# Shorter table steps, float64 pieces split by ScalarE and VectorE, and other first and last steps of the last layer

## The chip, the cores and the metric

The kernel runs on one core of a Trainium2 chip. The core has a matrix engine (TensorE, PE in the profile; its weight loads are PEld), a vector engine (VectorE, DVE), a scalar engine (ScalarE, ACT), a general engine (GpSimd, POOL), a queue engine that issues most of the transfers (SyncE, SP), and 16 DMA engines that all queues share. The metric is the device time of one execution in microseconds; lower is better. The kernel before takes 802.15 us (median of three runs, 800.84 to 803.86).

## The reference

Three layers follow each other. The first is clustered attention, which the change does not touch. Its output is a table x of 1536 tokens by 512 numbers. The second sends every token to the one expert of eight that its gate prefers. The third multiplies two projections and projects the product.

```python
logits = x @ w_gate                                  # 1536 x 8
expert_idx = np.argmax(logits, axis=1)
for e in range(8):
    xe = x[expert_idx == e]
    h = np.maximum(xe @ w1[e], 0.0)                  # 512 -> 1024
    out[mask] = gate_w[mask, None] * (h @ w2[e])     # 1024 -> 512
a, b = out @ w_a, out @ w_b                          # w_a, w_b, w_out are float64, 512 -> 1536
result = (a * b @ w_out).astype(np.float32)          # 1536 -> 512
```

The layer of experts is given in float32 and the last layer's weights in float64. The kernel keeps float32 accuracy with matmuls on shorter numbers: every operand is split into a high part and the rest (hi and lo, hh and hl, xh and xl, yh and yl), and three products hi·hi, hi·lo and lo·hi are added up.

## The kernel before

**Weights as pieces.** All weights come in pieces, in one list. A piece is loaded by SP into one of four buffers called raw (L102 for an expert's piece, L104 for a float64 one; 512 KB each). ScalarE casts it to hi (L138), and then raw − hi is lo (L142), computed by DVE for expert pieces of 128 x 1024 and by POOL for float64 ones of 128 x 512. A float64 piece first has its bits put together into float32 by three DVE operations (L121, L123, L125, into tmp, two buffers). The function `advance(n, engines, later)` takes the pieces up to number n through this path; with later = 1 the bits are made one piece ahead. A load of a piece is issued when the piece four places ahead has been passed on. Pieces 0 to 71 are the experts' (nine windows of eight pieces), numbers from 72 up are the last layer's. The list `chunk_src` gets an expert's pieces only once the registers that name the expert have been read.

**Windows.** The experts' work is nine windows, in an order that depends on the counts of tokens. The windows are 256 tokens long (`window`), but the fourth and the sixth run 128 tokens in another form (`tile_of`). A window has eight h groups (12 matmuls each, L1067; the results go to one of three PSUM banks, and hh by ScalarE and hl by DVE, L1072, set the bank free) and eight groups of y (L1082) into one buffer; at the end ScalarE and DVE each copy half of y to yt (L1090, L1091). Before a window, its tokens are fetched (xw, L1043), transposed on PE (xt, L1052) and split into xh and xl (L1055, L1056); the transposes of the next window stand between the y groups of this one.

**What sets the order.** The program is written out, and each engine takes its instructions in that order. `tick()` is called 16 times in a window, after each hl and before each y group; it counts t, runs one step of the tables if it is due, starts the second window's weights and tokens at t = 1, and calls `advance` up to a number that grows with t. The tables (a Python generator that stops at each yield) turn the counts of tokens into the order of the experts (`ri`, L659 to L674), the second kind of window (`wi`, L704) and the places of the tokens (`pu`, L767), for which POOL scatters `aux` (L769, twelve of them in two sets of six; each writes 128 rows of two words). Before, steps run at t = 0 to 3 and then, from t = 24, only in the second half of each window.

**Behind the windows** stands a loop (L1270) whose number of passes is read from the tables; it makes none here, but all engines meet at it. Then comes the last layer: 12 steps in a group, each with 24 matmuls into ab (L1354), the product ga, its split gh (L1362) and gl (L1363), and matmuls into four tiles o (L1377). Before each step `advance` takes the float64 pieces that it needs. At the end of the last group DVE adds up each tile's o to part (L1385) and POOL scatters it to the output (L1388). In the last group the tile t = 3 has the matmuls of its last two steps behind the three other tiles' ones.

The functions that the change touches, and their callers:

## Time and profile before

The profiled execution took 800.87 us, and its span (first to last instruction) is 799.1 us.

| what | value |
|---|---|
| runs | 803.86, 802.15, 800.84 us |
| profiled execution, its span | 800.87 us, 799.1 us |
| mean granted TensorE clock | 0.987 |
| PE busy | 766.6 us (96%) |
| DVE busy | 530.7 us (66%) |
| ACT busy | 356.1 us (45%) |
| POOL busy | 171.5 us (21%) |
| attention ends, experts begin | about 281 us |
| first to seventh window begin | 281.0, 310.4, 334.4, 357.7, 377.2, 401.0, 416.0 us |
| ninth window begins | 462.4 us |
| boundary with the loop, last layer | 487.6 to 499.5, 499.5 to 791.5 us |

The granted clock is a share of full speed: 1.00 is 2.4 GHz and half of it 1.2 GHz. The busy share of PE is high, but it is a mean over stages; where PE stands still is found by its waits and by stage.

### The profile page before, as it was taken

What the parts mean: (1) busy time and instruction counts of PE and PEld (TensorE: products, weight loads), DVE (VectorE), ACT (ScalarE), POOL (GpSimd) and SP (SyncE); (2) the same over time, 40 slices, a digit from 0 to 9 for tenths busy, and PEclk for the clock granted to TensorE, in tenths of its full rate; (3) what the DMA queues carried; (4) which work ended last, traced back from release to release, by engine and by line L of the source; (5) the groups of instructions that cost most, each with busy time, mean ns of one, the idle gap of its engine ahead of it and who ended that gap; (6) DMA issues with size and microseconds to landing.
All of it is one profiled execution on the core that took longest, in us unless ns stands there. A gap on an engine that the chain in (4) does not pass through costs nothing. (4 is left out here: it accounts for less than half of the span.)

```text
span 799.1 us, 12580 instructions
## 1 busy us (share of the span) xinstructions
PE 766.6 (96%) x4725; PEld 632.6 (79%) x4725; DVE 530.7 (66%) x939; ACT 356.1 (45%) x677; POOL 171.5 (21%) x172
## 2 busy tenths in 40 slices
PE   9999999999999889997999996999999999999996
PEld 8667666675666779996999986788888888888884
DVE  5877868868686787875776687856556665625332
ACT  6767667665675456455575532232241221211100
POOL 7533231414210400011300033312112111101011
PEclk9999999999999999999999998999999999999999
DMA  6585953855410268669997644413121230001011
GB/s 140 140 212 167 290 123 95 195 102 156 100 40 1 73 217 284 206 195 201 219 289 227 200 138 132 132 53 105 53 53 53 57 103 0 1 1 53 1 53 53
DMA packets 76302, 98.17 MB, mean 123 GB/s; under 512 B 28368, under 2 KB 49360, under 8 KB 76240
## 3 DMA queue, kind: packets, MB, share of 16 engines
q1 hardware_dynamic: 73792, 91.01, 41.6%
q0 software_dynamic: 2304, 6.31, 2.1%
q8 instruction: 38, 0.62, 0.3%
q14 instruction: 24, 0.20, 0.1%
q10 hardware_dynamic: 144, 0.03, 0.0%
HBM read 70.32 MB, written 10.50 MB: 101 GB/s over the span
## 5 line engine op out<-in xcount | busy, mean ns | idle before, releaser
L1354 PE MATMUL ab<-yh,hi 128*128 128x512 f32 x288 | 113.2, 393 | 6.5 <-ACT yh L1326 6.5
L1354 PE MATMUL ab<-yh,lo 128*128 128x512 f32 x288 | 113.0, 392 | 0.0
L1361 DVE TENSOR_TENSOR ga<-ga,ab 128x512 f32<-128x512 f32 x36 | 24.7, 685 | 127.3 <-PE ab L1354 104.4
L142 POOL TENSOR_TENSOR lo<-tmp,hi 128x512 fp32r<-128x512 f32 x36 | 51.6, 1433 | 247.6 <-ACT hi L138 245.6
L461 DVE TENSOR_REDUCE nm<-s 128x1 f32<-128x768 f32 x96 | 91.5, 953 | 18.2 <-PE s L459 11.3
L142 DVE TENSOR_TENSOR lo<-raw,hi 128x1024 fp32r<-128x1024 f32 x70 | 85.0, 1223 | 25.0 <-ACT hi L138 24.1
L468 ACT ACTIVATE pr<-s,nm 128x768 f32<-128x768 f32 x96 | 86.9, 905 | 18.3 <-DVE nm L461 16.3
L459 PE MATMUL s<-ks,qs 128*128 128x512 f32 (+1 forms) x384 | 91.6, 361 | 0.3 <-ACT pr L468 0.3
L482 PE MATMUL t<-ident,pr 128*128 128x128 f32 x576 | 82.8, 277 | 3.8 <-DVE pt L488 2.3
L1360 ACT COPY ga<-ab 128x512 f32<-128x512 f32 x36 | 21.1, 585 | 143.3 <-PE ab L1354 143.3
L482 PEld LDWEIGHTS t<-ident,pr 128*128 128x128 f32 x576 | 64.6, 141 | 25.1 <-issue 10.9
L138 ACT CAST hi<-raw 128x1024 fp32r<-128x1024 f32 x70 | 72.2, 1046 | 17.0 <-DMA raw<-in_moe_w 17.0
L1354 PE MATMUL ab<-yl,hi 128*128 128x512 f32 x288 | 77.3, 390 | 0.0
L498 PE MATMUL o<-pt,vn 128*64 128x384 f32 (+1 forms) x432 | 74.5, 468 | 0.0
L488 DVE COPY pt<-t 128x384 f32<-128x384 f32 x94 | 51.9, 552 | 27.2 <-PE t L482 27.0
L1354 PEld LDWEIGHTS ab<-yh,hi 128*128 128x128 f32 x288 | 54.6, 190 | 18.1 <-ACT yh L1326 6.7
L486 ACT COPY pt<-t 128x384 f32<-128x384 f32 x98 | 46.8, 479 | 46.6 <-PE t L482 43.8
L459 PEld LDWEIGHTS s<-ks,qs 128*128 128x128 f32 x384 | 58.5, 190 | 9.7 <-issue 4.4
L1082 PE MATMUL y<-hh,hi 128*128 128x256 f32 x224 | 64.1, 286 | 0.0
L1354 PEld LDWEIGHTS ab<-yh,lo 128*128 128x128 f32 x288 | 54.7, 190 | 11.3
L1354 PEld LDWEIGHTS ab<-yl,hi 128*128 128x128 f32 x288 | 54.5, 189 | 11.4
L1082 PE MATMUL y<-hh,lo 128*128 128x256 f32 x224 | 63.2, 282 | 0.0
(327 smaller groups left out, 1559.3 us busy)
## 6 DMA issues: line engine op xcount, KB each, us to landing
raw<-in_moe_w SPq DMA_DIRECT2D x72, 512.0 KB, 4.7
raw<-in_moe_w_a SPq DMA_DIRECT2D x12, 512.0 KB, 4.1
raw<-in_moe_w_b SPq DMA_DIRECT2D x12, 512.0 KB, 4.0
raw<-in_moe_w_out SPq DMA_DIRECT2D x12, 512.0 KB, 3.2
qs<-hiq SPq DMA_DIRECT2D x14, 384.0 KB
ks<-hik SPq DMA_DIRECT2D x28, 192.0 KB, 4.4
xs<-zero SPq DMA_DIRECT2D x8, 512.0 KB
xw<-xs SPq DMA_DIRECT2D x14, 256.0 KB, 3.7
```

The lines of the kernel that those rows point to most:

```text
L138: nc.scalar.copy(out=hi, in_=raw)
L142: eng.tensor_tensor(out=lo, in0=raw, in1=hi.bitcast(F32), op=ALU.subtract)
L459: nc.tensor.matmul(sc[:, c0:c1], lhsT=w, rhs=ks[s, h][:, i, c0:c1], start=(i == 0), stop=(i == 1))
L461: nc.vector.tensor_reduce(out=nm, in_=sc[:, 0:S], axis=AX.X, op=ALU.max, negate=True)
L468: nc.scalar.activation(out=pr, in_=sc[:, 0:S], func=AF.Exp, bias=nm, scale=1.0, accum_out=sums[p][:, t, h:h + 1])
L482: nc.tensor.transpose(x[:, 128 * n:128 * n + 128], pr[:, 128 * kb:128 * kb + 128], ident)
L486: nc.scalar.copy(out=dst, in_=src)
L488: nc.vector.tensor_copy(dst, src)
L498: nc.tensor.matmul(o[64 * h:64 * h + 64, 0:n], lhsT=vn[:, h, kb, :], rhs=pt_t[p, g, h][:, kb, 128 * j0:128 * j0 + n], start=(kb == 0), sto ...
L1082: nc.tensor.matmul(y[:, d, 0:n], lhsT=a_[:, fb % 2, 128 * d:128 * d + 128], rhs=b_[:, 0:n], start=(fb == 0 and d % 2 == 0 and i == 0), sto ...
L1354: nc.tensor.matmul(p_, lhsT=a_[:, d, f0:f0 + 128], rhs=b_[d], start=(i == 0), stop=(i == len(seq) - 1))
L1361: nc.vector.tensor_tensor(out=ga, in0=ga, in1=ab[1], op=ALU.mult)
```

## The change

Five parts, all in the order in which work is written out:

- The generator of the tables has eight more yields, so its steps are shorter, and one step runs at every tick from t = 0 on. The second window's weights and tokens are started at t = 4 and no longer at t = 1. The pieces of the experts lead by t // 8, not t // 4 (up to the same bound). In the first window the second window's transposes stand behind the y groups 3 and 5, not 1 and 3.
- The float64 pieces before the loop are eight, not nine. They are made at eight ticks listed in WHEN64, counted from t = T64 = 122, by `split_ahead`: bits on DVE, hi on ScalarE, and lo on DVE, one piece behind the hi.
- `held` bounds the loads before the last layer.
- In the first group of the last layer the pieces of a step are bounded by min(n64, 10 + step * 15 // 11 − (step == 0)); gh and gl have three buffers.
- In the last group, the last tile's matmuls of step GF − 3 also go behind those of the other tiles, so 9 of its matmuls stand there and no longer 6.

The diff, cut to what matters (the other yields are like the two shown):

```diff
--- before.py
+++ after.py
@@ -129,15 +129,18 @@
     def piece_parts(n, hi_eng, lo_eng):
-        raw = bits_t.pop(n)
+        raw = bits_t.pop(n) if lo_eng else bits_t[n]
         i, j = pieces[n]
         hi, lo = hi_t[i], lo_t[i]
         if i >= MOE2:
             hi, lo = (x[:, CH // 2 * j:CH // 2 * j + CH // 2] for x in (hi, lo))
         if hi_eng == "act":
             nc.scalar.copy(out=hi, in_=raw)
-        else:
+        elif hi_eng:
             nc.vector.tensor_copy(hi, raw)
+        if not lo_eng:
+            return
         eng = nc.gpsimd if lo_eng == "pool" else nc.vector
         eng.tensor_tensor(out=lo, in0=raw, in1=hi.bitcast(F32), op=ALU.subtract)
@@ -649,12 +652,15 @@
         e1 = cp.tile([128, E], F32, name="we1")
         od = tp.tile([128, E], F32, name="od")
         nc.vector.tensor_reduce(out=m[:, 0:1], in_=cnt[:, 1:E], axis=AX.X, op=ALU.min)
+        yield
         nc.vector.scalar_tensor_tensor(out=e1[:, 1:E], in0=cnt[:, 1:E], scalar=m[:, 0:1], in1=efirst[:, 0, 1:E],
                                        op0=ALU.is_le, op1=ALU.mult)
         nc.vector.tensor_reduce(out=m[:, 1:2], in_=e1[:, 1:E], axis=AX.X, op=ALU.max)
+        yield
         nc.vector.tensor_scalar(out=m[:, 2:3], in0=m[:, 1:2], scalar1=-1.0, scalar2=float(E), op0=ALU.mult, op1=ALU.add)
         nc.vector.scalar_tensor_tensor(out=od, in0=ecol, scalar=m[:, 2:3], in1=ecol, op0=ALU.is_ge, op1=ALU.add)
         nc.vector.tensor_copy(od[:, E - 1:E], m[:, 2:3])
+        yield
         ri = tp.tile([128, 3, E], I32, name="ri")
         nc.vector.tensor_copy(ri[:, 0, :], od)
         nc.vector.tensor_scalar(out=ri[:, 1, :], in0=od, scalar1=float(NTOK), scalar2=None, op0=ALU.mult)
@@ -1005,6 +1015,10 @@
     pools["b"] = pb
     st_me = ExitStack()
     mp = pool(st_me, "moe")
+    LAST64 = 8
+    held = [True]
     nload = [NA + NRAW]
     nsplit = [NA]
     nparts = [NA]
@@ -1023,6 +1037,21 @@
         while later and nsplit[0] < n:
             first_part()
+    def split_ahead(n):
+        if nparts[0] < MOE2:
+            advance(MOE2, ENG)
+        while nsplit[0] < n:
+            i = nsplit[0]
+            first_part()
+            piece_parts(i, "act", None)
+            if i > MOE2:
+                piece_parts(i - 1, None, "dve")
+                nparts[0] = i
+        if n == MOE2 + LAST64 and nparts[0] < n:
+            piece_parts(n - 1, None, "dve")
+            nparts[0] = n
     def first_part():
         i = nsplit[0]
         piece_bits(i)
@@ -1031,7 +1060,8 @@
             load_ahead(nsplit[0])
     def load_ahead(n):
-        while nload[0] < min(len(pieces), n + NRAW) and pieces[nload[0]] in chunk_src:
+        most = MOE2 + LAST64 + NRAW if held[0] else len(pieces)
+        while nload[0] < min(most, n + NRAW) and pieces[nload[0]] in chunk_src:
             piece_load(nload[0])
             nload[0] += 1
@@ -1055,7 +1085,7 @@
         nc.scalar.copy(out=oh, in_=xv)
         nc.vector.tensor_tensor(out=ol, in0=xv, in1=oh.bitcast(F32), op=ALU.subtract)
-    def window(w, n, c0, tick, nxt=None):
+    def window(w, n, c0, tick, nxt, at):
         hh, hl = [], []
         y = mps.tile([128, DB, W], F32, tag="y", name=f"y{w}")
         for fb in range(FB):
@@ -1082,8 +1112,8 @@
                     nc.tensor.matmul(y[:, d, 0:n], lhsT=a_[:, fb % 2, 128 * d:128 * d + 128], rhs=b_[:, 0:n],
                                      start=(fb == 0 and d % 2 == 0 and i == 0),
                                      stop=(fb == FB - 1 and d % 2 == 1 and i == 2), skip_group_check=True)
-            if nxt is not None and fb in (1, 3):
-                nxt(fb // 2)
+            if fb in at:
+                nxt(at.index(fb))
         return y
     def store(y, n, at):
@@ -1165,22 +1195,23 @@
     ENG = [("act", "dve")]
     ENG64 = [("act", "pool")]
-    T64 = 2 * (MOE2 - NSLOT + 2)
+    T64 = 2 * (MOE2 - NSLOT + 1)
+    WHEN64 = (1, 3, 5, 8, 11, 14, 16, 17)
     def tick():
         t = state["t"]
-        if t < 4 or t >= 24 and t % 16 >= 8:
-            next(tab_steps, 0)
-        if t == 1:
+        next(tab_steps, 0)
+        if t == 4:
             start_next(0)
-        n = t // 2 + min(LEAD + t // 4, NSLOT - 2)
-        if n > MOE2:
-            n = MOE2 + (t - T64) * 3 // 5
-        if n > MOE2 and t < 16 * (E + 1) - 3:
-            advance(n, ENG64, 1)
-        elif n <= MOE2:
-            advance(n, ENG)
+        n = t // 2 + min(LEAD + t // 8, NSLOT - 2)
+        n64 = sum(t - T64 >= o for o in WHEN64)
+        if n64:
+            split_ahead(MOE2 + n64)
+        else:
+            advance(min(n, MOE2), ENG)
         state["t"] += 1
     advance(NA + AN, ENG)
@@ -1257,7 +1288,7 @@
         if r >= E - 1:
             finish = tile_of(r, 8 * pos, tick, nxt, lambda r=r: ov[r])
         else:
-            y = window(r, W, 8 * pos, tick, nxt)
+            y = window(r, W, 8 * pos, tick, nxt, (1, 3) if pos else (3, 5))
             store(y, W, ov[r])
     keep_warm(2, "xt", [128, 512], 2, mps)
     st_me.close()
@@ -1333,6 +1364,7 @@
     NGR = FB2 // GF
+    held[0] = False
     y_next = split_y(0, 0)
     for gr in range(NGR):
         for st in range(NST):
@@ -1343,7 +1375,8 @@
                 fb = GF * gr + fl
                 if fl < GF:
                     step = GF * st + fl
-                    advance(MOE2 + 2 * max(3 * (fb // 2) + 4, 6 * gr + 6 + (step + 1) // 2), ENG64, 1)
+                    n64 = 2 * max(3 * (fb // 2) + 4, 6 * gr + 6 + (step + 1) // 2)
+                    advance(MOE2 + (min(n64, LAST64 + 2 + step * 15 // 11 - (step == 0)) if gr == 0 else n64), ENG64, 1)
                     f0 = 128 * (fb % 2)
                     ab = []
                     for i2 in range(2):
@@ -1355,8 +1388,8 @@
                                              start=(i == 0), stop=(i == len(seq) - 1))
                         ab.append(p_)
                     ga = bp.tile([128, YN], F32, tag="ga", name=f"ga{st}_{fb}", bufs=2)
-                    gh = bp.tile([128, YN], F32R, tag="gh", name=f"gh{st}_{fb}", bufs=2)
-                    gl = bp.tile([128, YN], F32R, tag="gl", name=f"gl{st}_{fb}", bufs=2)
+                    gh = bp.tile([128, YN], F32R, tag="gh", name=f"gh{st}_{fb}", bufs=3)
+                    gl = bp.tile([128, YN], F32R, tag="gl", name=f"gl{st}_{fb}", bufs=3)
                     nc.scalar.copy(out=ga, in_=ab[0])
                     nc.vector.tensor_tensor(out=ga, in0=ga, in1=ab[1], op=ALU.mult)
                     nc.vector.tensor_copy(gh, ga)
@@ -1367,9 +1400,9 @@
                 late = [YT - 1] if (gr, st) == (NGR - 1, NST - 1) else []
                 for t in range(YT):
-                    if fl == GF - 1 and t in late or fl == 0:
+                    if fl in (GF - 2, GF - 1) and t in late or fl == 0:
                         continue
-                    for fo in range(fl - 1 - (fl == GF and t in late), fl):
+                    for fo in range(fl - 1 - 2 * (fl == GF and t in late), fl):
                         f = GF * gr + fo
                         wh, wl = parts(MOE2 + 3 * (f // 2) + 2, 2)
                         gh, gl = g_t[fo]
```

On DVE, in the first window behind the hl of its first h group, stood the following before. The names cnts, wm, we and od are the tables' counts and orders, ri the order of the experts that SP reads, hl_1 the second h group's rest.

```order
L646 COPY cnts<-cnt 128x8
L651 TENSOR_REDUCE wm<-cnts 128x1
L652 SCALAR_TENSOR_TENSOR we_3494<-cnts,wm,efirst 128x7
L654 TENSOR_REDUCE wm<-we_3494 128x1
L655 TENSOR_SCALAR wm<-wm 128x1
L656 SCALAR_TENSOR_TENSOR od<-ecol,wm 128x8
L657 COPY od<-wm 128x1
L659 CAST ri<-od 128x8
L660 TENSOR_SCALAR ri<-od 128x8
L1072 SCALAR_TENSOR_TENSOR hl_1_3519<-h_1_3505,hh_1_3518 128x256
```

Now, on DVE at the same place, lo is a piece of an expert.

```order
L1102 SCALAR_TENSOR_TENSOR hl_1_3511<-h_1_3497,hh_1_3510 128x256
L656 SCALAR_TENSOR_TENSOR we_3494<-cnts,wm,efirst 128x7
L658 TENSOR_REDUCE wm<-we_3494 128x1
L1102 SCALAR_TENSOR_TENSOR hl_2_3530<-h_2_3516,hh_2_3529 128x256
L660 TENSOR_SCALAR wm<-wm 128x1
L661 SCALAR_TENSOR_TENSOR od<-ecol,wm 128x8
L662 COPY od<-wm 128x1
L145 TENSOR_TENSOR lo_3537<-raw_3444,hi_3536 128x1024
L1102 SCALAR_TENSOR_TENSOR hl_3_3554<-h_3_3540,hh_3_3553 128x256
L665 CAST ri<-od 128x8
L666 TENSOR_SCALAR ri<-od 128x8
```

The two rows that make ri came before hl_1; now hl_1, hl_2, one lo and hl_3 stand ahead of them.

On DVE before the loop, at the end of the last window, stood these rows. tmp are the bits of a float64 piece (one raw number is one piece), and yt is the copy of y.

```order
L121 TENSOR_SCALAR tmp_6068<-raw_5934 128x512
L123 SCALAR_TENSOR_TENSOR tmp_6068<-raw_5934,tmp_6068 128x512
L125 SCALAR_TENSOR_TENSOR tmp_6068<-raw_5934,tmp_6068 128x512
L121 TENSOR_SCALAR tmp_6100<-raw_5976 128x512
L123 SCALAR_TENSOR_TENSOR tmp_6100<-raw_5976,tmp_6100 128x512
L125 SCALAR_TENSOR_TENSOR tmp_6100<-raw_5976,tmp_6100 128x512
L121 TENSOR_SCALAR tmp_6122<-raw_6020 128x512
L123 SCALAR_TENSOR_TENSOR tmp_6122<-raw_6020,tmp_6122 128x512
L125 SCALAR_TENSOR_TENSOR tmp_6122<-raw_6020,tmp_6122 128x512
L1205 TENSOR_LOAD ri
L1091 ISA
L1091 COPY yt<-y_5883 128x2x256
```

Now the rows on DVE before the loop are these; lo is the rest of a float64 piece.

```order
L121 TENSOR_SCALAR tmp_6091<-raw_5884 128x512
L123 SCALAR_TENSOR_TENSOR tmp_6091<-raw_5884,tmp_6091 128x512
L125 SCALAR_TENSOR_TENSOR tmp_6091<-raw_5884,tmp_6091 128x512
L145 TENSOR_TENSOR lo_6014<-tmp_6057,hi_6013 128x512
L121 TENSOR_SCALAR tmp_6111<-raw_5958 128x512
L123 SCALAR_TENSOR_TENSOR tmp_6111<-raw_5958,tmp_6111 128x512
L125 SCALAR_TENSOR_TENSOR tmp_6111<-raw_5958,tmp_6111 128x512
L145 TENSOR_TENSOR lo_6090<-tmp_6091,hi_6089 128x512
L145 TENSOR_TENSOR lo_6090<-tmp_6111,hi_6089 128x512
L1236 TENSOR_LOAD ri
L1121 ISA
L1121 COPY yt<-y_5902 128x2x256
```

The bits of three pieces stood ahead of the copy yt; now two pieces' bits stand there, the lo of the pieces stand among them, and the last two rows ahead of the copy are the lo of the seventh and the eighth piece.

On DVE, the first pu (the index of a set of six scatters of aux, which POOL issues behind it) stood before at the end of the third window, just ahead of that window's copy of y to yt.

```order
L757 TENSOR_TENSOR dl<-offs,erow 128x8
L142 TENSOR_TENSOR lo_4465<-raw_4314,hi_4464 128x1024
L761 TENSOR_TENSOR pt_4482<-ohe_135,dl 128x48
L763 TENSOR_REDUCE ps_4484<-pt_4482 128x6
L765 TENSOR_TENSOR ps_4484<-ps_4484,slot_137 128x6
L767 CAST pu_4499<-ps_4484 128x6
L142 TENSOR_TENSOR lo_4505<-raw_4354,hi_4504 128x1024
L1091 ISA
L1091 COPY yt<-y_4212 128x2x256
```

Now, on DVE, it stands behind the last hl of the second window (hl_7); xl are the third window's tokens.

```order
L1102 SCALAR_TENSOR_TENSOR hl_7_4063<-h_7_4049,hh_7_4062 128x256
L767 TENSOR_TENSOR dl<-offs,erow 128x8
L771 TENSOR_TENSOR pt_4068<-ohe_135,dl 128x48
L773 TENSOR_REDUCE ps_4070<-pt_4068 128x6
L145 TENSOR_TENSOR lo_4073<-raw_3906,hi_4072 128x1024
L145 TENSOR_TENSOR lo_4079<-raw_3951,hi_4078 128x1024
L775 TENSOR_TENSOR ps_4070<-ps_4070,slot_137 128x6
L777 CAST pu_4097<-ps_4070 128x6
L1086 TENSOR_TENSOR xl_4115<-xt_0_4116,xh_4114 128x4x128
L145 TENSOR_TENSOR lo_4127<-raw_4002,hi_4126 128x1024
L1236 TENSOR_LOAD ri
L1086 TENSOR_TENSOR xl_4115<-xt_1_4163,xh_4114 128x4x128
```

The first pu has moved ahead by one window. The second one, which stood at the start of the fifth window's h groups, now stands behind the third window's hl_0, so it has moved by two.

## Rows read from the trace of the kernel before

**Rows 1.** Waits of PE, 280 to 520 us: total, times, longest (us).

```profile
PE ab L1354 <- ACT yh L1326: 6.5, 1, 6.5
PE h L1067 <- DVE hl L1072: 4.2, 5, 1.8
PE xt L1052 <- issue: 3.9, 1, 3.9
...
PE o L1377 <- DVE gl L1363: 0.4, 1, 0.4
```

**Rows 2.** The same view of the last window, 462 to 488 us.

```profile
PE h L1067 <- DVE hl L1072: 1.6, 2, 1.4
```

**Rows 3.** Stages: length, busy PE, PEld, DVE, ACT, POOL, PEclk, DMA, GB/s.

```profile
281.00:310.40 29.40, 26.66 (x201) 25.70 (x202) 25.17 (x57) 17.07 (x25) 0.84 (x1) 0.94 0.75 235
...
357.70:377.20 19.50, 15.38 (x90) 13.10 (x90) 9.92 (x13) 10.54 (x16) 5.39 (x5) 0.91 0.93 206
377.20:401.00 23.80, 23.80 (x200) 23.76 (x200) 17.16 (x26) 13.42 (x21) 7.91 (x6) 1.00 0.90 228
...
487.60:499.50 11.90, 5.39 (x17) 4.20 (x17) 7.57 (x11) 2.25 (x4) 2.70 (x2) 0.71 0.38 92
499.50:791.50 292.00, 291.56 (x1285) 240.73 (x1283) 159.09 (x242) 61.00 (x107) 46.65 (x37) 1.00 0.16 49
```

**Rows 4.** Timeline of DVE, first window: start, duration (us), engine, line, work.

```profile
286.37 0.16 DVE L646 COPY cnts<-cnt 128x8 f32<-128x8 f32 x1
...
287.93 0.16 DVE L660 TENSOR_SCALAR ri<-od 128x8 int32<-128x8 f32 x1
...
292.09 1.23 DVE L142 TENSOR_TENSOR lo<-raw,hi 128x1024 fp32r<-128x1024 f32 x1
293.23 0.42 DVE L1072 SCALAR_TENSOR_TENSOR hl<-h,hh 128x256 fp32r<-128x256 f32 x1
293.56 0.16 DVE L695 SCALAR_TENSOR_TENSOR wrs<-cnts,cap 128x8 f32<-128x8 f32 x1
```

**Rows 5.** Timelines of SP and of ACT, first window (idle before, releaser).

```profile
290.65 20.62 SPq L102 DMA_DIRECT2D raw<-in_moe_w  x12
...
296.12 1.04 ACT L138 CAST hi<-raw 128x1024 fp32r<-128x1024 f32 x1 [4.59 <-DMA raw<-in_moe_w]
```

**Rows 6.** Timeline of PE, second window.

```profile
311.44 0.64 PE L1067 MATMUL h<-xl,hi 128*128 128x256 f32 x4
...
319.19 0.28 PE L1067 MATMUL h<-xh,hi 128*128 128x256 f32 x1
```

**Rows 7.** Timeline of POOL, third to fourth window.

```profile
355.87 1.70 POOL L769 DMA_INDIRECT aux<-auxt,pu  x1 [74.03 <-DVE pu L767]
```

**Rows 8.** Three microseconds of the fourth window, columns as in rows 3.

```profile
364.00:367.00 3.00, 2.77 (x13) 2.00 (x13) 1.98 (x3) 1.78 (x4) 0.48 (x1) 1.00 0.49 53
```

**Rows 9.** Waits of ACT, 377 to 402 us.

```profile
ACT hi L138 <- DMA raw<-in_moe_w: 1.5, 3, 0.8
```

**Rows 10.** All instructions of line 123: ns min, median, max.

```profile
L123 DVE SCALAR_TENSOR_TENSOR tmp<-raw,tmp x36: 691/693/1668, 460.0 to 684.1; 128x512 uint32<-128x512 uint32 x36
```

**Rows 11.** Groups of DVE by line and form, 464 to 490: us, mean ns, idle.

```profile
L121 DVE TENSOR_SCALAR tmp<-raw 128x512 uint32<-128x512 uint32 x8 | 3.3, 415 | 0.0
```

**Rows 12.** Timelines of DVE and of SP at the boundary.

```profile
489.24 0.68 DVE L1091 COPY yt<-y 128x512 f32 x1
494.15 0.76 DVE L1324 CAST yh<-yt 128x512 fp32r<-128x512 f32 x2 [4.23 <-SPq L1270]
...
489.35 0.38 SPq L104 DMA_DIRECT2D raw<-in_moe_w_a  x1
```

**Rows 13.** DMA issues (page): KB each, us from issue to landing.

```profile
raw<-in_moe_w_a SPq DMA_DIRECT2D x12, 512.0 KB, 4.1
```

**Rows 14.** Timelines of DVE and of POOL at the end.

```profile
791.58 0.75 DVE L1385 SCALAR_TENSOR_TENSOR part<-o,ai,part 128x512 f32<-128x512 f32 x1 [0.61 <-PE o L1377]
...
793.71 0.97 POOL L1388 DMA_INDIRECT out<-part,ai  x1 [0.30 <-issue]
```

4 lines of the change are left out of this document (added).

## The prediction

> **What bounds the kernel now.** I began with the clocks and the span: 799.1 us in the profiled execution, which took 800.87 (the three timed runs have a median of 802.15, 1.28 more). The page gives TensorE (PE) 766.6 us of work in that span, so at most some 30 us can be won by letting it work, and the question is where it stands still or runs at half clock. The view of waits, taken from 280 to 520 us, where the change acts, answers the first half: 6.5 us before the last layer's first matmul, 3.9 before one set of transposes, 4.2 in five waits of h matmuls for VectorE's (DVE) hl, and 0.4 for gl [rows 1]. Of the 4.2, 1.6 lie in the last window [rows 2], so 2.6 lie in the first. The second half stands in the view by stage: granted clock 0.94 over the 29.4 us of the first window, 0.91 over the 19.5 us of the fourth, 0.71 over the 11.9 us of the boundary [rows 3]. A clock of 0.94 over 29.4 us is 0.06 × 29.4 = 1.8 us of lost full speed, 0.91 over 19.5 us again 1.8; the low level (1.2 GHz) follows each of the long waits. In the last layer PE is busy 291.56 of 292.00 us: only its start and its end can change. So five places carry the forecast.
>
> **A, first two windows: +2.6 us.** DVE runs 25 small table operations between 286.37 and 293.56, with three hl and one lo of an expert piece among them; lo takes 293.23 − 292.09 = 1.14, hl 293.56 − 293.23 = 0.33, so a table operation takes (7.19 − 3 × 0.33 − 1.14) / 25 = 0.20 [rows 4]. In long steps they delay hl and with it PE by 2.6 us and 1.8 of clock: together −4.4 if short steps were all. But `ri`, the expert order, is what the second window's loads wait for. It is ready at 288.09, and its first load is issued at 290.65 (2.56 later, behind two loads of xw), and the cast of that piece starts at 296.12, 5.47 after the issue [rows 4, 5]. After the change three hl and one lo stand ahead of `ri` which stood behind it: 3 × 0.33 + 1.14 = 2.13 later, so loads at 292.8, the first cast at 298.3, its end (1.04) at 299.3. DVE runs in order, and the lo of that piece stands ahead of everything that comes later; the operations that would have filled the wait are behind it. From 299.4 it must do five lo (5.7), one hl (0.33), the 27 remaining table operations of the window (5.4) and the second window's two xl (half a lo each, 1.14): 12.6, so 312.0, where PE wants xl at 311.44 [rows 6]. From there to the hl that frees the bank of the second window's seventh h group: four lo 4.6, a store 0.7, four hl 1.3, sixteen table operations 3.2, so 321.8, against 319.19 when PE starts that group now [rows 6]. The three h banks and the y half before it give no more slack. I therefore take it that the gain of 4.4 in the first window is used up, and that the stream leaves the second 2.6 us later. The bounds: −4.4 if the loads are not missed, and +4.1 if the whole delay of the loads (2.13) also falls on the clock (1.8) at one more stop.
>
> **B, fourth window: −5.6, and +1.3 elsewhere.** PE waits 3.89 us there for transposes [rows 1], and ScalarE and DVE are idle as well, because the pieces are late. Just before it POOL issues six scatters of `aux`, from 355.87, 128 rows of eight bytes each [rows 7]; what all queues move falls to 53 GB/s from 364 to 367 us [rows 8], where the stage's mean is 206 [rows 3]. This window has half the tokens of the others, so it takes its 4 MB of weights in the shortest time of all and has no reserve. With one table step per tick, the first six follow the second window's last hl and the second six the third window's first one: they are out of the fourth window, which gives 3.9 of wait and 1.8 of clock, −5.7; I take −5.6. What do they cost where they go? The six that already fall in a full window, the fifth, cost PE nothing: it is busy 23.80 of 23.80 us [rows 3], and ScalarE waited 1.5 us in three for loads [rows 9]. A full window has 23 us for the same 4 MB. So I charge +0.8 for the third window and +0.5 for what the late stream leaves to the fourth; the bounds are 0 (the fifth window) and 5.6 (the stall moves whole).
>
> Here the Trainium skill, "DMA: Bandwidth & Descriptors", section "Issuing engines are not separate DMA queues", says that transfers started from any engine end on the same 16 DMA engines and interleave. The collapse to 53 GB/s agrees. By that rule alone, moving the scatters frees nobody; it moves the queueing to whatever loads are then under way, which is the second rival below. Its "Specifications" add that pieces under 512 bytes cost a read and a write back; no row here shows that apart from the drop itself.
>
> **C, last window: −1.2.** Its 1.6 us of waits for hl [rows 2] come behind the integer operations that make the bits of the float64 pieces: their second step has a shortest time of 691 ns, a median of 693 and a longest of 1668 [rows 10], while the first takes 415 [rows 11]. I read the long ones as slowed by POOL's subtract, which runs beside them. With lo on DVE, POOL has nothing to do there. A piece now takes DVE three bit operations (0.42 + 0.69 + 0.69, the third taken like the second) and one lo of half width (0.57), 2.4 us; eight make 19.0 us, and eight hl add 2.6: 21.6 in a window that, like the fifth, lasts 23.8 where nothing waits [rows 3]. That fits, so I leave 0.4 of the 1.6. Bounds: −1.6, and +0.8 where the two-microsecond margin is gone and the two last lo (1.1) push the boundary.
>
> **D, the boundary: −5.0.** DVE copies its half of y to `yt` at 489.24, late behind the bits of three pieces; SP issues the thirteenth load at 489.35, and DVE is then held 4.23 us by SP's loop entry, to 494.15 [rows 12]. Such a load lands 4.1 us after its issue [rows 13]: 493.4, and the loop is entered only then. Before the loop there are now twelve loads, not thirteen; the last waits for the bits of the eighth piece, not the ninth, and these are made some 4 us before the end of y. It then lands about when y ends. DVE's copy starts at once, about 1 us sooner. Of the 6.5 us of wait about 2 to 3 are the copy, the barrier and the splits of y, which stay; −4 of wait, −1 of clock (0.71 over 11.9 us, 3.4 lost in all, most of it while nothing ran). Bounds: −1.5, if most of the 4.23 is the loop's own, and −5.5.
>
> **E and F: −0.4 and −0.7.** The wait for gl at the last layer's start [rows 1] goes with one piece's bits instead of three and a third buffer: −0.4; the bounds are −0.4 and +1.0, if a piece that is now split later is missed. No row of the first steps waits for a piece, so I charge nothing for that. At the end POOL's four output scatters follow each other: the fourth starts at 793.71, though its tile is ready at 791.58 + 0.75 = 792.33 [rows 14]. Three matmuls of the last tile move behind the others, so tiles 0 to 2 are ready 3 × 291.56 / 1285 = 0.68 sooner [rows 3]; the fourth scatter could start at 793.03, still after 792.33. Bounds 0 and −0.7.
>
> **Sum.** +2.6 − 5.6 + 1.3 − 1.2 − 5.0 − 0.4 − 0.7 = −9.0. 800.87 − 9.0 = 791.9 for a profiled execution; with half to all of the 1.28 that the median is above it, 792.6.
>
> **Rivals.**
> 1. The late loads cost nothing and the first windows keep their gain: A is −4.4 and not +2.6, so 792.6 − 7.0 = 785.6. For it: four buffers hold pieces that the second window takes 15 us later. Against it: DVE's order above. 0.15.
> 2. The scatters' stall moves whole into the third window (the rule above): 5.6 − 1.3 more, 796.9. For it: the first six fall while the late loads of A are still being caught up. Against it: the fifth window. 0.20.
> 3. The loop's entry does not change (the count of loads is not what it waits for, and the hold binds nothing, since the pieces stop at eight anyway): D is −1.5, so 796.1. For it: the only view of the wait names SP's loop line itself. Against it: the landing time fits to 0.7 us. 0.10.
> 4. Slower: DVE becomes the bound of the first windows. All of the 55 or so table operations behind the seventh tick (55 × 0.20 = 11.0) then come behind the late lo, and the 5.5 us wait for the first load is exposed on DVE; if nothing of it is hidden, PE loses 16.5 us where 2.6 are charged, and the result is 792.6 + 13.9 = 806.5. It decides from the point where DVE's backlog passes what the three h banks hold: from 311.44 to 319.19 PE goes through five groups and the end of one [rows 6], about 1.5 us each, so 4.5 us. Against it: a part of these operations falls in the y halves, where PE waits for no result of DVE. 0.07.
>
> **How the numbers follow.** The forecast has 0.48: its own range is 789 to 796. What a measurement of this kernel can tell from no change is about 0.5%, 4 us: faster is under 798.1, slower over 806.2. Forecast and rivals 1, 2 and 3 are faster except for the upper part of 2 and 3: 0.79. Within 0.5%: 0.14, from 2 and 3 together and a mild form of 4. Slower: 0.07, the hard form of 4. The range 786.0 to 799.0 leaves out most of rival 4 and half of rival 1.
>
> **What would show it.** A: `ri` is ready about 2 us later, the cast after it starts near 298.3, and hl waits appear in the second window. B: no wait of 3 us before the transposes of the fourth window, POOL's scatters between 326 and 347. C: the second bit operation no longer reaches 1.66 us before the loop. D: the wait for yh is under 3 us and SP's last load ahead of the loop is issued well before y ends. E: no wait for gl. F: the fourth output scatter 0.7 us after the third's end is gone, the distance from the last matmul to the end of the span shorter by 0.7. Wrong is the whole if PE waits over 5 us in the second and third window together, or if the yh wait stays at 6 us.

## The result and the profile after

The changed kernel takes 794.36 us (median of four, 791.79 to 795.91), the kernel before beside it 801.5 us: a ratio of 0.9905 with a 95% interval of 0.9882 to 0.9928. A second measurement on another chip gave 794.76 against 801.44, 0.9911 (0.9876 to 0.9945). The forecast was 792.6, in a range of 786 to 799.

The first profiled execution took 791.79 us, the fastest of the four, with a span of 789.7 at a mean clock of 0.995. Its distance to the profile of before is larger than that of the medians: the first expert window begins at 279.45 us where it began at 281.20, and that 1.75 us lies in the attention, which the change does not touch. So I count from the first h matmul of the first window; a window's length is from its first h matmul to that of the next. The end of y and the last matmul are each counted to the start of that matmul. In the kernel before the seventh window begins at 414.4 us and the sixth takes 13.25 us; the 416.0 given ahead of the forecast is wrong. The third column of numbers is the changed kernel's second profile.

| stage (us) | before | after | second profile | forecast of the difference |
|---|---|---|---|---|
| first and second window | 29.28 + 23.89 | 24.69 + 30.07 | 24.93 + 31.00 | A +2.6 |
| third and fourth | 23.39 + 19.48 | 25.69 + 17.39 | 25.09 + 17.66 | B −4.3 |
| fifth to eighth | 85.21 | 84.52 | 84.53 | 0 |
| ninth, up to the end of y | 24.97 | 23.65 | 23.65 | C −1.2 |
| from there to the first matmul of the last layer | 7.24 | 3.25 | 3.17 | D −5.0, with the next row |
| from there to the first o matmul | 13.04 | 11.27 | 12.65 | |
| from there to the last matmul | 283.45 | 282.72 | 282.75 | E −0.4 |
| from there to the end | 7.95 | 6.98 | 6.95 | F −0.7 |
| sum of the differences | | −7.7 | −5.5 | −9.0 |

The waits of PE in the profile after, 275 to 520 us (total, times, longest), answer to [rows 1]:

```profile
PE h L1097 <- DVE xl L1086: 3.9, 1, 3.9
PE h L1097 <- DVE hl L1102: 3.7, 5, 1.5
PE ab L1387 <- ACT yh L1357: 2.5, 1, 2.5
PE ht L1148 <- ACT hs L1143: 2.4, 1, 2.4
```

The wait for yh has shrunk from 6.5 to 2.5, and the one for the transposes xt (3.9) is gone; in the second profile 1.9 us of it are left. In their place stand a wait for xl in the second window, which did not exist, and one for ht in the fourth. The waits of PE in the second window, and behind the dots in the third:

```profile
PE h L1097 <- DVE xl L1086: 3.9, 1, 3.9
PE h L1097 <- DVE hl L1102: 0.5, 1, 0.5
...
PE h L1097 <- DVE hl L1102: 2.0, 2, 1.5
```

Together they are 6.4 us. The forecast named over 5 us there as the sign that it is wrong as a whole, so by its own sign its account of these windows fails, although the time lies in its range.

By stage, as in [rows 3] (first, second, third, fourth window, boundary):

```profile
279.40:304.10 24.70, 24.22 (x201) 23.86 (x201) 18.80 (x51) 14.11 (x21) 0.69 (x1) 1.00 0.68 219
304.10:334.20 30.10, 25.71 (x202) 25.27 (x201) 26.90 (x69) 15.39 (x23) 3.97 (x4) 0.94 0.71 221
334.20:359.90 25.70, 23.65 (x199) 23.24 (x198) 13.03 (x21) 11.77 (x19) 10.28 (x9) 1.00 0.89 157
359.90:377.30 17.40, 14.99 (x91) 13.13 (x90) 13.05 (x16) 12.61 (x18) 0.00 (x0) 0.90 0.91 305
...
485.70:498.00 12.30, 9.78 (x45) 7.71 (x44) 8.65 (x16) 2.94 (x5) 1.29 (x1) 1.00 0.24 53
```

The stop and the clock of 0.94 have moved from the first window into the second, and the fourth still runs at 0.90. The chain of the forecast's step A can be followed on DVE, SP, ACT and PE (timelines, [rows 4 to 6] before):

```profile
288.04 0.16 DVE L666 TENSOR_SCALAR ri<-od 128x8 int32<-128x8 f32 x1
...
296.70 1.23 DVE L145 TENSOR_TENSOR lo<-raw,hi 128x1024 fp32r<-128x1024 f32 x1 [4.70 <-ACT hi L139]
...
308.54 0.69 DVE L1086 TENSOR_TENSOR xl<-xt,xh 128x512 fp32r<-128x512 f32 x1 [0.49 <-DVE wcum L728]
...
290.76 20.86 SPq L102 DMA_DIRECT2D raw<-in_moe_w  x10
...
295.62 1.05 ACT L139 CAST hi<-raw 128x1024 fp32r<-128x1024 f32 x1 [4.43 <-DMA raw<-in_moe_w]
...
309.29 0.74 PE L1097 MATMUL h<-xl,hi 128*128 128x256 f32 x4 [3.94 <-DVE xl L1086]
```

Counted from the first h matmul, `ri` is ready 8.75 us in (288.20 − 279.45; before 6.89), the load goes out 1.86 us later than it did, DVE stands still for 4.70 us, and xl ends late.

The scatters, on POOL, now run in the third window and just ahead of it (timeline, [rows 7] before):

```profile
329.32 0.97 POOL L779 DMA_INDIRECT aux<-auxt,pu  x1 [49.22 <-DVE pu L777]
...
347.94 0.97 POOL L779 DMA_INDIRECT aux<-auxt,pu  x1 [0.30 <-issue]
```

Two stretches of 4 us of the third window, as in [rows 8], and the waits of ACT from 334.2 to 377.3, as in [rows 9]:

```profile
341.00:345.00 4.00, 2.58 (x21) 2.58 (x22) 3.53 (x6) 2.14 (x5) 3.09 (x4) 1.00 1.06 91
...
353.00:357.00 4.00, 4.00 (x37) 4.00 (x36) 0.14 (x1) 1.23 (x2) 0.00 (x0) 1.00 0.86 118
```

```profile
ACT hi L139 <- DMA raw<-in_moe_w: 10.9, 8, 4.4
```

In these two stretches the DMA engines are busy and the loads are slow (91 and 118 GB/s, where the first window has 219), the second time up to 9 us after the last scatter was issued; from 337 to 341 us, where the first set ends and the second begins, they get 223. Casts wait 10.9 us for loads in the two windows. The boundary on DVE and SP ([rows 12] before), and then all instructions of the second bit operation ([rows 10]):

```profile
485.78 0.69 DVE L1121 COPY yt<-y 128x512 f32 x1 [1.46 <-PE y L1112]
488.22 0.76 DVE L1355 CAST yh<-yt 128x512 fp32r<-128x512 f32 x2 [1.75 <-SPq L1301]
...
480.45 2.86 SPq L104 DMA_DIRECT2D raw<-in_moe_w_out  x2
```

```profile
L123 DVE SCALAR_TENSOR_TENSOR tmp<-raw,tmp x36: 691/693/694, 457.6 to 675.6; 128x512 uint32<-128x512 uint32 x36
```

DVE is now free 1.46 us before y ends, its wait at the loop is 1.75 us where it was 4.23, and the last loads ahead of the loop are issued more than 2 us before y ends. At the end ([rows 14]) POOL's last scatter starts 1.46 us after the start of DVE's last sum, where it was 2.13:

```profile
783.12 0.75 DVE L1418 SCALAR_TENSOR_TENSOR part<-o,ai,part 128x512 f32<-128x512 f32 x1 [1.29 <-PE o L1410]
...
784.58 0.98 POOL L1421 DMA_INDIRECT out<-part,ai  x1 [0.30 <-issue]
```

### The profile page after: what moved, and what is told of

Same layout as the page of the kernel before. It is cut to its first block, busy times and chain, and to the rows that moved or that the text cites. A ratio compares the mean times of both kernels' runs of the same rounds, so it can differ in the third digit from the quotient of the medians.

```text
span 789.7 us, 12580 instructions
## 1 busy us (share of the span) xinstructions
PE 760.3 (96%) x4725; PEld 628.5 (80%) x4725; DVE 523.5 (66%) x947; ACT 356.5 (45%) x677; POOL 157.6 (20%) x164
## 5 line engine op out<-in xcount | busy, mean ns | idle before, releaser
L145 POOL TENSOR_TENSOR lo<-tmp,hi 128x512 fp32r<-128x512 f32 x28 | 38.3, 1366 | 292.9 <-ACT hi L139 292.9
L491 DVE COPY pt<-t 128x384 f32<-128x384 f32 x94 | 51.9, 552 | 24.9 <-PE t L485 24.6
```

The lines of the kernel that those rows point to most:

```text
L145: eng.tensor_tensor(out=lo, in0=raw, in1=hi.bitcast(F32), op=ALU.subtract)
L491: nc.vector.tensor_copy(dst, src)
```

## The experiments

Differences are given to the kernel before, measured on the same chip, or by stage to a profile. The chips differ by some 3 us for the same kernel, so times of different rounds are compared by ratio.

**The first part alone (e1).** The kernel before with the shorter steps at every tick, the start at tick 4, the lead and the later transposes:

```diff
...
-        if t < 4 or t >= 24 and t % 16 >= 8:
-            next(tab_steps, 0)
-        if t == 1:
+        next(tab_steps, 0)
+        if t == 4:
...
```

> The kernel before with the first part of the change alone: shorter table steps at every tick, start of the second window at tick 4, lead t // 8, later transposes in the first window. Theory (the tables' part moves time and wins nothing): the two first windows together 1.6 us longer than before (53.2 to 54.8 us), the third and the fourth together unchanged within 1 us (42.9 us), so 801 to 803 us where the kernel before takes 801.5. Rival (the forecast's terms A and B as they stand, +2.6 and -4.3, the rest of what the changed kernel shows there being caused by its other parts): 799 to 800 us, with the fourth window near 14.5 us.

Measured: 801.19 against 799.83, a ratio of 1.0017 (0.9996 to 1.0039). The windows are 24.69, 29.89, 25.45 and 16.12 us, 96.15 together where the kernel before has 96.04. This part moves the lost time and wins nothing.

**All but the first part (e2).** The changed kernel with that part taken back.

> The changed kernel with the first part taken back: steps of the tables, start of the second window, lead and transposes as before; the eight float64 pieces on DVE and ACT, the first steps and the end of the last layer as changed. Theory (nearly the whole gain is made from the last window on): 793.0 to 795.5 us, the wait of the last layer's first matmul for yh 2 to 3 us, the fourth window again with a wait of some 3.9 us for its transposes (19.5 us long). Rival (the tables' part gives half of the gain, by the scatters that leave the fourth window): 797 to 799 us.

Measured: 791.26 against 799.83, 0.9890 (0.9857 to 0.9923). From the end of y to the first matmul it takes 3.27 us, as in the changed kernel; the first two windows are again 29.27 and 23.89, the fourth 18.37. The whole gain is here, as the theory had it, and its interval overlaps that of the changed kernel.

**Scatters later (e3).** The changed kernel, with the two sets at the start of the seventh and the eighth window:

```diff
+        for _ in range(70):
+            yield
         yield from gates(B - 1, True)
...
         for b in range(B):
+            for _ in range(10 * b):
+                yield
```

> The changed kernel, but the steps of the tables that make pu and issue the twelve scatters of aux come 70 and 80 ticks later, so that POOL scatters in the seventh and the eighth window. Theory (the scatters slow the loads, and the change has only moved that from the fourth window to the third and the fourth): the third window goes from 25.7 to about 23.5 us, the fourth from 17.4 to 13.3 to 15 us, the seventh and the eighth grow by under 1 us; 788.5 to 791 us where the changed kernel takes 794.4. Rival (the third and the fourth window are late because the second window's loads start 1.9 us later and the four buffers hand this on): both stay at 25.7 and 17.4 within 0.7 us, and the time stays at 794 us. A third way, that the scatters cost the same wherever they are: 25.7 + 17.4 shrink as in the theory, the seventh and the eighth window grow by 4 us, and the time stays at 794 us.

Measured: 791.18 against 799.83, 0.9890 (0.9857 to 0.9922). The view by stage, third and fourth window, then the seventh, eighth and ninth up to the last layer's first matmul:

```profile
335.80:359.00 23.20, 23.20 (x198) 23.18 (x198) 14.90 (x19) 12.61 (x19) 0.00 (x0) 1.00 0.72 231
359.00:372.30 13.30, 13.29 (x90) 11.88 (x90) 10.78 (x14) 11.49 (x17) 0.00 (x0) 1.00 0.78 267
...
409.10:434.20 25.10, 24.74 (x206) 24.30 (x205) 18.92 (x34) 13.91 (x22) 8.08 (x6) 1.00 0.82 224
434.20:458.30 24.10, 23.75 (x203) 23.55 (x201) 15.05 (x23) 12.12 (x19) 7.54 (x6) 1.00 0.87 204
458.30:488.10 29.80, 24.94 (x197) 24.55 (x197) 22.80 (x42) 8.61 (x19) 0.00 (x0) 0.94 0.46 146
```

Without scatters the third and the fourth window run without a stop, 36.5 us where the changed kernel has 43.1, though the second window is as late as ever (30.04). So the scatters, and not the late loads, cost 6.6 us there, 2.5 in the third window and 4.1 in the fourth. Where they went, 4.3 us come back: 0.9 in the seventh window, 0.5 in the eighth, and 2.9 in the ninth, where PE waits 2.3 us for hl and its clock falls to 0.94. That the ninth window pays for the scatters of the eighth is read from the order and was not tried by a run. The price is between the theory (under 1 us each) and the third way (4 us each); the theory had not reckoned with the window after the scatters. By the runs, 0.9890 cannot be told from the changed kernel's 0.9905.

**The order of experts first (e6).**

```diff
-        next(tab_steps, 0)
-        if t == 4:
+        for _ in range(5 if t == 0 else 1):
+            next(tab_steps, 0)
+        if t == 1:
```

> The changed kernel, but the first five table steps, up to the order of the experts that the second window's loads wait for, run in one go at tick 0, and the second window is started at tick 1 as before. All later steps stay short. Theory (the late start of the loads is what the first two windows lose by): the second window's first load is issued 1.9 us sooner, counted from the first h matmul, DVE's long wait ends that much sooner, the 3.9 us wait for xl in the second window falls to 1 to 2.5 us, half clock behind it included a gain of 2 to 4 us, and some 0.5 us is lost in the first window as hl of the second group comes 2 us later: 791 to 793 us where the changed kernel takes 794.4. Rival (DVE has too much to do in these two windows, whenever the loads start): the wait for xl stays within 0.7 us of 3.9, 793.5 to 795 us.

Measured: 790.73 against 799.83, 0.9897 (0.9841 to 0.9953). The waits of PE, 275 to 520 us, and the two first windows by stage:

```profile
PE h L1097 <- DVE hl L1102: 5.6, 5, 2.0
...
PE h L1097 <- DVE xl L1086: 1.7, 1, 1.7
```

```profile
278.90:304.50 25.60, 24.51 (x202) 23.95 (x203) 23.32 (x73) 15.28 (x22) 0.59 (x1) 1.00 0.69 226
304.50:333.70 29.20, 25.62 (x203) 25.22 (x202) 23.72 (x49) 14.56 (x22) 9.52 (x9) 0.94 0.76 205
```

The wait for xl falls to 1.7 as the theory had it, and the loads do start sooner; but a wait for hl of 1.8 us takes its place, and the two windows take 54.8 us as in the changed kernel. The rival has the time right (no gain here), the theory the wait. The third and the fourth window take 40.1 us instead of 43.1. The scatters also stand sooner in this kernel, but that they are the cause is not shown, and by the runs this kernel cannot be told from the changed one.

**lo on POOL (e4).** In `split_ahead`, "dve" becomes "pool".

> The changed kernel with lo of the eight float64 pieces before the loop back on POOL, at the same place in the program. Theory (the forecast's term C: POOL's subtract beside DVE's integer operations makes these 1.66 us long, and hl and the copy to yt come late behind them): the longest second bit operation before the loop is 1.66 us again instead of 0.69, the last window up to the end of y takes 24.6 to 25.2 us instead of 23.65, and from there to the first matmul of the last layer 3.3 to 4.8 us instead of 3.25: 795.5 to 797.5 us where the changed kernel takes 794.4. Rival (the last window gained because pieces come at other ticks and are one fewer, not by the engine of lo): 23.5 to 23.9 us and 3.3 us, 794 to 795 us.

Measured: 793.43 against 798.06, 0.9936 (0.9914 to 0.9958), inconclusive beside the changed kernel's 0.9905. By the profile the ninth window takes 24.01 us up to the end of y, and 3.17 from there. Groups of DVE by form, 462 to 489 us:

```profile
L125 DVE SCALAR_TENSOR_TENSOR tmp<-raw,tmp 128x512 uint32<-128x512 uint32 x8 | 8.5, 1057 | 0.3
L123 DVE SCALAR_TENSOR_TENSOR tmp<-raw,tmp 128x512 uint32<-128x512 uint32 x8 | 5.5, 693 | 0.3
```

It is the third bit operation, not the second, that is slow here, and only for three of the eight pieces (a mean of 1057 ns, where 0.69 us is the short and 1.66 the long form). In the kernel before each of the eight pieces had one long operation (three times L123, five times L125). So at the new ticks POOL's subtract meets DVE's bit operations less often, and this run does not put a price on those meetings as they were before. Of the 1.32 us that the ninth window gained, lo on DVE gives 0.36; 0.96 come by the other ticks, with five meetings fewer, and by the one piece fewer, which no run separates. Neither the theory's 24.6 nor the rival's 23.9 was met.

In this profile the third and the fourth window take 48.6 us, 5.5 more than in the changed kernel's, though up to the eighth window the two programs are the same. The profiled execution is the slowest of the ten, 798.87 us. PE waits for the transposes xt again, and casts wait 17.6 us for loads in the two windows, not 10.9:

```profile
PE xt L1082 <- issue: 3.7, 1, 3.7
...
ACT hi L139 <- DMA raw<-in_moe_w: 17.6, 8, 4.0
```

So what the scatters cost differs from one execution to the next; what decides it stays open.

**One load held (e5).** The kernel before, with the thirteenth load issued behind the loop:

```diff
-        while nload[0] < min(len(pieces), n + NRAW) and pieces[nload[0]] in chunk_src:
+        most = MOE2 + 8 + NRAW if held[0] else len(pieces)
+        while nload[0] < min(most, n + NRAW) and pieces[nload[0]] in chunk_src:
...
+    held[0] = False
+    load_ahead(nsplit[0])
```

> The kernel before, with one load moved: the thirteenth float64 load, which it issues just ahead of the loop, is issued behind it. Nothing else is changed, nine pieces' bits and POOL's subtracts stay. Theory (the forecast's term D: the loop is entered only when the last load before it has landed): from the end of y to the first matmul of the last layer 4.3 to 5.3 us instead of 7.24, where DVE's copy stays late behind the bits, and the half clock behind it is shorter: 797.5 to 799.5 us where the kernel before takes 801.5. Rival (the wait is the loop's own entry, or only DVE's late copy): 6.9 to 7.4 us, 801 to 802 us.

Measured: 796.12 against 798.06, 0.9970 (0.9945 to 0.9994). From the end of y to the first matmul it takes 3.92 us instead of 7.24. PE's waits there, from 482 to 520 us:

```profile
PE ab L1358 <- ACT yh L1328: 3.2, 1, 3.2
PE o L1381 <- DVE gl L1367: 1.1, 1, 1.1
PE ab L1358 <- DVE yl L1332: 0.8, 1, 0.8
```

One load, moved past the loop, gives 3.3 of the 4.0 us, more than the theory had. That the landing was the wait can be read in the kernel before: the traffic of that load ends between 492.6 and 493.0 us (the last two numbers of a row are the DMA engines' share and GB/s), and ScalarE and DVE go on at 493.99 and 494.15.

```profile
492.20:492.60 0.40, 0.00 (x0) 0.00 (x0) 0.00 (x0) 0.00 (x0) 0.00 (x0) 0.50 0.86 328
492.60:493.00 0.40, 0.00 (x0) 0.00 (x0) 0.00 (x0) 0.00 (x0) 0.00 (x0) 0.50 0.09 31
```

That the remaining 0.7 us are DVE's late copy is not shown. Of the 3.3 us a quarter, 0.8, is given back in waits for gl and yl in the first steps (297.28 us from the first matmul of the last layer to the last one, before 296.49).

**Buffers and the end alone (e8).** The kernel before with `bufs=3` for gh and gl and the nine late matmuls.

> The kernel before with three buffers for gh and gl and with three more of the last tile's matmuls behind the other tiles; all else as before. Theory (terms E and F as forecast): the wait of 0.4 us for gl in the first steps goes by the third buffer, the first of the four output scatters starts 0.7 us sooner, and from the last matmul to the end of the span it is 6.9 to 7.0 us instead of 7.95: together 1.0 to 1.7 us, 799.8 to 800.5 us where the kernel before takes 801.5. Rival (the wait for gl goes only where fewer pieces are made in the first steps): 0.7 to 1.0 us from the end alone.

Measured: 797.53 against 798.06, 0.9999 (0.9981 to 1.0017): nothing that can be told. By the profile the end takes 7.27 instead of 7.95, and from the last layer's first matmul to its last 296.48 instead of 296.49. The end gives its 0.7. The wait of 0.4 us for gl is gone from the list, as the theory had it, but the stage is no shorter, so the buffers alone give nothing, as the rival had it.

**More pieces in the first steps (e12).** The changed kernel with the old line for the pieces of a step.

```diff
-                    advance(MOE2 + (min(n64, LAST64 + 2 + step * 15 // 11 - (step == 0)) if gr == 0 else n64), ENG64, 1)
+                    advance(MOE2 + 2 * max(3 * (fb // 2) + 4, 6 * gr + 6 + (step + 1) // 2), ENG64, 1)
```

> The changed kernel with the number of float64 pieces in the first steps of the last layer as before; three buffers of gh and gl stay. Theory (the forecast's term E, in that the wait for gl comes from the pieces that DVE makes ahead of it, and the third buffer alone does not take it away): the last layer from its first matmul to the end grows by 0.4 to 0.9 us, with a wait of PE for gl in the first steps; 794.8 to 795.3 us where the changed kernel takes 794.4. Rival (fewer pieces cost or win nothing here): within 0.2 us. A third way, larger than forecast: DVE, with ten pieces to make at once, holds PE for 2 us or more.

Measured: 798.77 against 801.44, 0.9972 (0.9953 to 0.9991), where the changed kernel on the same chip has 0.9911. Its waits of PE behind the boundary, 482 to 530 us:

```profile
PE o L1409 <- DVE gh L1394: 2.4, 1, 2.4
PE o L1409 <- DVE gl L1395: 1.2, 1, 1.2
```

From the first to the last matmul of the last layer it takes 299.84 us, in the changed kernel's second profile 295.40. The third way is right: four pieces' bits in a row, from 491.6 to 501.7 us, stand ahead of ga on DVE. There are four because eight pieces are made ahead of the loop; in the kernel before and in e5 it was nine, and three were left for this place.

**The changed kernel again (e10).**

> The changed kernel itself, once more, on the chip of the two runs that follow. Theory: against the kernel before a ratio of 0.987 to 0.993, and the same stages as in the first profile within 0.3 us up to the second window (24.7 and 30.1 us), the third and fourth together 42 to 44 us. Rival (the third and fourth window depend on how the scatters meet the loads in one execution): their sum differs by 2 us or more from the 43.1 us of the first profile while the first two windows agree.

Its stages stand in the table above. The second window is 0.9 us longer than in the first profile, where the theory allowed 0.3; the third and the fourth together are 42.75, in the first profile 43.08. These two profiles agree and do not show the rival's spread; the 48.6 us of e4, with the same program up to there, do. The rival is not out.

**Steps in the y halves (e9).** Short steps up to tick 6, the rest in the second halves from tick 24 on. By the trace the scatters then run in the fifth window (368.9 to 378.5 us) and in the seventh (405.6 to 414.2 us):

```diff
-        next(tab_steps, 0)
+        if t < 7 or t >= 24 and t % 16 >= 8:
+            next(tab_steps, 0)
...
+        for _ in range(5):
+            yield
         yield from gates(B - 1, True)
...
         for b in range(B):
+            for _ in range(9 * b):
+                yield
```

> The changed kernel with the order of experts made at ticks 0 to 6 in short steps as changed, but all later table steps only in the second half of each window from tick 24 on, and the two sets of scatters just ahead of the fifth and of the seventh window. Theory (what the second window loses, 30.1 us instead of 23.9, is table work that DVE does behind the late loads; what the third and the fourth lose is the scatters): first window 24.7 us as changed, second 24 to 27 us, third 23.3 to 24, fourth 13.3 to 14.5, fifth and seventh up to 1 us longer than changed: 782 to 786 us where the changed kernel takes 794.4. Rival (the late loads themselves cost the second window its 6 us): second window 28.5 to 30.5 us, the rest as in the theory, 786 to 789 us.

Measured: 781.13 against 798.06, 0.9803 (0.9767 to 0.9838). By stage, first, second and sixth window:

```profile
277.50:302.20 24.70, 24.24 (x201) 23.89 (x202) 17.73 (x36) 14.11 (x21) 0.70 (x1) 1.00 0.68 219
302.20:326.70 24.50, 24.07 (x202) 23.70 (x201) 21.80 (x48) 15.43 (x22) 0.00 (x0) 1.00 0.83 273
...
388.40:403.40 15.00, 13.33 (x90) 11.70 (x89) 11.51 (x14) 11.73 (x17) 0.00 (x0) 1.00 0.86 290
```

The order of experts comes at the same ticks as in the changed kernel, and the second window's first load goes out as late (11.31 us behind the first h matmul in both), yet the second window takes 24.5 us instead of 30.1. DVE works 21.8 us in it and not 26.9. The theory holds, and this version beats both kernels. The set in the fifth window is paid in the fifth (24.46 us, in the changed kernel 23.55) and in the short sixth (15.02 instead of 13.26). The set in the seventh is paid nowhere: the seventh and the eighth take 24.15 and 23.56 us, as in the changed kernel, where no scatters run there.

**Scatters one by one (e11).** As e9, but with twelve single scatters, five ticks apart, from the fifth window on: pu is cast column by column.

> The order of experts in short steps at ticks 0 to 6, the later table steps in the second half of each window up to tick 55, and then the twelve scatters one at a time, five ticks apart (pu is cast column by column), from the fifth window to the eighth. Theory (six scatters in a row stop the loads for longer than four buffers cover, one alone does not): no wait of PE in the windows three to eight, which take 23.4, 13.3, 23.6, 13.3, 24.2 and 23.6 us, so 1.5 to 3.5 us less than with two sets ahead of the fifth and the seventh window, a ratio to the kernel before of 0.975 to 0.979. Rival (each scatter costs the same wherever it is): the sum of these windows stays within 1 us of the 124.4 us measured with two sets, a ratio of 0.979 to 0.982.

Measured: 788.32 against 801.44, 0.9832 (0.9797 to 0.9867). The windows three to eight sum to 124.7 us, with two sets 124.4. By its number the rival holds: spreading the scatters wins nothing. Its reason does not: the six scatters that run in the seventh and the eighth window cost nothing there (again 24.15 and 23.56 us), and the six in the fifth and the sixth cost 2.2 us.

## Why the forecast was right, and where it was not

The time was right, 1.8 us off, and in part by luck. The terms at the boundary and behind it held; the one large miss, 4.5 us in B, is offset in the first profile by 1.0 in A, 1.5 in C to F and 0.7 that was not forecast: −7.7 for −9.0. In the second profile less offsets it, and −5.5 is left.

- **A (+2.6; measured +1.6 and +2.8).** The size held, and so did the chain on DVE: `ri` 1.9 us late (forecast 2.1), the wait of DVE, xl late. (The upper bound of +4.1 is a slip, 2.13 + 1.8 is 3.9; both measurements lie inside it.) The cause was given the wrong weight. An earlier start of the loads moved nothing (e6: 54.8 us), while table work put elsewhere gave 5.6 us with the loads as late as in the changed kernel (e9). So it was the mild form of rival 4: too much work for DVE in these two windows. Rival 1 is out, but late loads by themselves cost little: with loads as late, and less table work, the first two windows of e9 take 49.2 us, 4.0 less than before.
- **B (−5.6 + 1.3; measured +0.2 and −0.1).** This is the step that failed: the price of the scatters in their new place, put at 1.3 us after the fifth window of before. The 3.9 us wait for xt did go from the fourth window in the first profile, but by e3 the scatters cost 6.6 us in the changed kernel's third and fourth window, where they cost 6.4 before (42.87 − 36.46). Rival 2 has the amount; the place it names, the third window, has 2.5 of it and the fourth 4.1. The Trainium skill's rule ("DMA: Bandwidth & Descriptors", section "Issuing engines are not separate DMA queues"), that transfers run on the same 16 DMA engines whichever engine started them, agrees: the casts wait for the loads under way, 10.9 us in these two windows. It does not give the price for PE, and this ranges widely: two sets cost 6.6 us here and 4.3 in e3, and of e9's two sets the first cost 2.7 and the second nothing. My error was to take a price from one window of one execution. In another execution of before's order the same set in the fifth window was not free: e8 has 24.25 and 14.59 us for the fifth and the sixth window, the profile of before 23.88 and 13.25. What decides the price is not shown; in e8, e9 and e11 the short sixth window pays most of it, in e6 the full third.
- **C (−1.2; measured −1.3).** Right in size. Of the cause, POOL's subtract, e4 shows 0.36; how much of the rest is the same subtract, meeting fewer bit operations at the new ticks, is open.
- **D (−5.0; measured −5.8 and −4.5 with the first products).** Right, and by the mechanism named: e5 moves one load and gets 3.3 us. Rival 3 is out. The two profiles differ in the clock: the first stays at 1.00 over the boundary, and the second has a stretch at the low level, 11.27 against 12.65 us up to the first o. The second is the usual one: e2, e3, e4, e6 and e11 have 12.6 to 12.7 us there, only e9 has 11.4.
- **E (−0.4; measured −0.7) and F (−0.7; measured −1.0).** Right in sign. E was mis-read as a small gain: with eight pieces made ahead of the loop and not nine, the old bound leaves four for the first step, and these cost 4 to 5 us (e12); three cost 0.8 more than before in e5, where the loop is also entered sooner. So this part is what the smaller number ahead of the loop needs. e8 shows that the third buffer does nothing by itself. In F the 0.7 is shown by e8. The other 0.3 comes and goes: e4 and e11, with the changed kernel's end, take 7.3 us there and not 7.0.
- **Not forecast:** the fifth to eighth window, −0.7, of which 0.3 lie in the fifth, which lost its scatters.

That `held` binds nothing was argued from the code and not tried by a run.

## What to carry to other kernels

Small transfers that are moved to another place in the same stream of loads may be paid again there or one window later, and one window of one profile does not tell the price: here a set of six scatters cost from nothing to 6.4 us. Look at the window after the one where they run, and put them where it is not a short one. When less is made ahead of a boundary, ask how much then falls in the first step behind it: three pieces there cost 0.8 us more in e5, four cost 4 to 5 in e12. A wait that goes when its cause is made earlier, and comes back as another wait on the same engine, says that the engine is full; then only taking work out of that stretch helps.

## What the hardware showed that was not expected

Of a piece's three bit operations on DVE the second and the third, with two inputs of 128x512 in SBUF, took 0.69 us alone and 1.66 us where POOL's subtract was already running as they began. One that had begun before the subtract kept its 0.69. In the last window and the last layer of the kernel before, all 24 DVE operations of this shape that began while the subtract ran were long, and all 120 others short, gl and yl included. One piece of it, on POOL and then on DVE:

```profile
468.42 1.80 POOL L142 TENSOR_TENSOR lo<-tmp,hi 128x512 fp32r<-128x512 f32 x1 [2.00 <-PE h L1067]
...
468.39 0.69 DVE L123 SCALAR_TENSOR_TENSOR tmp<-raw,tmp 128x512 uint32<-128x512 uint32 x1
469.12 1.66 DVE L125 SCALAR_TENSOR_TENSOR tmp<-raw,tmp 128x512 uint32<-128x512 uint32 x1
```

So one operation of a piece pays the whole, and the other nothing. The first operation, with one such input, took 0.41 to 0.43 us, but in e4 the two that began while the subtract ran took 0.53 and 0.67. For two inputs that agrees with the Trainium skill ("SBUF — State Buffer", section "Who interferes with whom"), by which a DVE instruction with two SBUF inputs contends with a GpSimd instruction that reads SBUF, and the order of issue decides which of them waits. And a loop that makes no pass still held the engines until the load issued ahead of it had landed: 3.3 us for one load of 512 KB (e5).
